# A cached-attention decode kernel: the output projection moved behind the last V piece, V sums gathered before they are turned, and one V piece loaded in two row ranges

## The chip, the cores and the metric

One NeuronCore of a Trainium2 chip; one launch. Times are device microseconds (us) of whole executions. Most are medians of 4 to 9 runs, taken in turns with the kernel before on the same chip. A program on one core has no second core to compare with, so single looks have an unknown state; all the runs behind a median were fast ones, and the granted TensorE clock is given where it matters.

## The reference

A decode step with a key/value cache (B = 4, one query token each, 32 heads, 8192 cached keys, head size 128, bf16), mixed by a gate with a small expert layer:

```python
q = (x @ wq)                                  # 4 x 32 heads x 128
scores = einsum("bhqd,bhkd->bhqk", q, k_cache) * 128**-0.5
p = softmax(scores)
o = einsum("bhqk,bhkd->bhqd", p, v_cache)
a = o.reshape(B, 1, 32 * 128) @ wo            # the output projection, wo is 4096 x 1024
b = x + scattered gated MLP(x)                # B_w_gate, B_w_up, B_w_down
out = g * a + (1 - g) * b
```

The caches K and V are 268 MB each. Everything is read once: 575.7 MB in all.

## The kernel before

K and V stream through a ring of five SBUF buffers in pieces of 4 MB (two heads of one batch entry, 128 partitions x 32 KB). There are NT = 64 K pieces and 64 V pieces; V trails K by LAG = 4. `V[NT-1]` below is the last V piece.

```python
HT = 2; JR = 128; GT = 4; GH = 8; NT = 64; LAG = 4; RING = JR * Dh      # 16384 elements
ring = ctx.enter_context(tc.tile_pool(name="ring", bufs=5))
...
def kv_view(cache, u):
    b, h0 = heads(u)
    return cache[b, h0:h0 + HT].rearrange("h (r j) d -> (h r) (j d)", j=JR)   # 128 rows of 32 KB
...
def v_piece(u):
    ...
    vn = slot()                                   # the next ring buffer
    vv = kv_view(A_v_cache, u)
    cut = 4 if u == NT - 1 else 1                 # the last piece comes in 4 column cuts
    for c in range(cut):
        lo, hi = c * RING // cut, (c + 1) * RING // cut
        nc.sync.dma_start(out=vn[:, lo:hi], in_=vv[:, lo:hi])
    o_ps = ops.tile([NM, 4 * Dh], F32, name="o_ps")            # NM = 8 rows
    ...                                           # 32 matmuls of 128x512 into o_ps
    o_sb = osp.tile([NM, 4 * Dh], F32, name="o_sb")
    nc.scalar.copy(out=o_sb[:], in_=o_ps[:])
    def finish():                                 # turn this piece's sums
        ...
        for q in range(4):
            nc.tensor.matmul(oT[:, HT * t:HT * t + HT], lhsT=o_sb[:, q * Dh:(q + 1) * Dh],
                             rhs=ident[0:NM, q:NM:4], start=(q == 0), stop=(q == 3))
        if t == GT - 1: ...                       # every 4th piece: scale into OT
    pending.append(finish)                        # run inside the next piece
...
GE = NWB - GH // WB                               # 6 of 8 row groups of wo, known before the last group
GS = GE // 2 + 1                                  # 4
for u in range(NT + LAG):
    if u < NT: k_piece(u)
    if u == NT + 1:
        flush(); o_rows(0, GE)
        wo_piece(0, GS)()                         # 4 MB of wo, between V[NT-4] and V[NT-3]
    if u >= LAG: v_piece(u - LAG)
    ...
early = wo_piece(GS, GE)                          # 2 MB, loaded behind V[NT-1]
late = [wo_piece(GE, NWB - 1), wo_piece(NWB - 1, NWB, 0, FR - 1), wo_piece(NWB - 1, NWB, FR - 1, FR)]
flush(); early(); o_rows(GE, NWB)
for use in late: use()
...                                               # acc -> res -> out
```

`wo_piece` issues a load and returns the matmuls that use it (8 of 128x512 per row group); `o_rows` turns finished heads into the projection's stationary rows.

Of the kernel before, what the change touches and what calls it, by code (L numbers as in the profile page):

```python
# [10 lines left out]
F32 = mybir.dt.float32  # L11
U32 = mybir.dt.uint32
ACT = mybir.ActivationFunctionType
ALU = mybir.AluOpType
# [5 lines left out]
def kernel(  # L20
# [22 lines left out]
    nc = tc.nc  # L43
    P = 128
    Bn, Sq, D = A_x.shape
    _, H, Sk, Dh = A_k_cache.shape
    F = B_w_gate.shape[1]
    DT = D // P
    HT = 2
    JR = Sk * HT // P  # L50
    JC = JR // 16
    GT = 4
    GH = GT * HT
# [3 lines left out]
    NT = Bn * H // HT  # L57
    LAG = 4
    FR = 4
# [3 lines left out]
    RING = JR * Dh  # L63
# [6 lines left out]
    const = ctx.enter_context(tc.tile_pool(name="const", bufs=1))  # L70
    ring = ctx.enter_context(tc.tile_pool(name="ring", bufs=5))
    ttp = ctx.enter_context(tc.tile_pool(name="ttp", bufs=2))
    ptp = ctx.enter_context(tc.tile_pool(name="ptp", bufs=2))
    osp = ctx.enter_context(tc.tile_pool(name="osp", bufs=2))
    stat = ctx.enter_context(tc.tile_pool(name="stat", bufs=3))
    shrp = ctx.enter_context(tc.tile_pool(name="shrp", bufs=1, space=PSUM))
    accp = ctx.enter_context(tc.tile_pool(name="accp", bufs=1, space=PSUM))
# [1 line left out]
    ops = ctx.enter_context(tc.tile_pool(name="ops", bufs=2, space=PSUM))  # L79
    o2p = ctx.enter_context(tc.tile_pool(name="o2p", bufs=1, space=PSUM))  # L80

    def slot():
        return ring.tile([P, RING], BF, name="piece", tag="piece")
# [11 lines left out]
    ident = const.tile([P, P], F32)  # L95
# [11 lines left out]
    for he in range(4):  # L107
        half, e = divmod(he, 2)
        nc.gpsimd.affine_select(out=R[:, he, :], in_=R[:, he, :], compare_op=ALU.not_equal, fill=1.0,  # L109
                                base=-(64 * half + e), pattern=[[0, 4], [-2, 32]], channel_multiplier=1)  # L110
# [3 lines left out]
                            base=0, pattern=[[-JC, GT], [-32, NQ]], channel_multiplier=1)  # L114
    nc.gpsimd.affine_select(out=m32[:], in_=m32[:], compare_op=ALU.is_ge, fill=0.0,
                            base=JC - 1, pattern=[[JC, GT], [32, NQ]], channel_multiplier=-1)
# [3 lines left out]
    nc.vector.tensor_scalar(out=pen8[:], in0=mask8[:], scalar1=-1.0, scalar2=3.0e38, op0=ALU.add, op1=ALU.mult)  # L120
    nmask8 = const.tile([P, GH], F32)
    nc.vector.tensor_scalar(out=nmask8[:], in0=mask8[:], scalar1=-scale, scalar2=None, op0=ALU.mult)
    ZW = 31 + P + 1
    Zt = [const.tile([P, 4, ZW], BF, name=f"Z{i}") for i in range(2)]
    PB = [const.tile([P, 32, 4, HT, 4], BF, name=f"PB{i}") for i in range(2)]
    for z in Zt + PB:
        nc.gpsimd.memset(z[:], 0.0)  # L127

    qT = const.tile([P, H, Bn], BF)
# [1 line left out]
    OT = const.tile([P, H, Bn], BF)  # L131
    LT = const.tile([P, FR, H // FR, Bn], BF)
    hT = const.tile([P, FG, FR, Bn], BF)
    sgb = const.tile([P, 2, Bn], F32)
# [10 lines left out]
    def mm_acc(out_ap, lhsT, rhs, start=False):  # L145
        nc.tensor.matmul(out_ap, lhsT=lhsT, rhs=rhs, start=start, stop=True, skip_group_check=True)  # L146
# [67 lines left out]
    NWB = H // WB  # L214

    def o_rows(g0, g1):

        n = g1 - g0
        lp = ops.tile([P, FR, n, Bn], F32, name="o_ps")
        for k in range(WB):  # L220
            for r in range(FR):
                nc.tensor.matmul(lp[32 * k:32 * k + 32, r], lhsT=identb[:, r:P:FR],
                                 rhs=OT[:, WB * g0 + k:WB * g1:WB, :], start=True, stop=True, skip_group_check=True)
        nc.vector.tensor_copy(out=LT[:, :, g0:g1, :], in_=lp[:])

    def wo_piece(g0, g1, r0=0, r1=FR):
        ng, nr = g1 - g0, r1 - r0
        w = slot()[:, :ng * nr * D].rearrange("p (g r n) -> p g r n", g=ng, r=nr)
        nc.sync.dma_start(out=w.rearrange("p g r n -> p g (r n)"),
                          in_=wov[:, g0:g1, r0:r1].rearrange("p g r n -> p g (r n)"))  # L230

        def use():
            for g in range(ng):
                for r in range(nr):
                    for n in range(NH):
                        mm_acc(acc[:, n * NB:(n + 1) * NB], LT[:, r0 + r, g0 + g, :], w[:, g, r, n * NB:(n + 1) * NB])
        return use
# [1 line left out]

    S_ps = {}  # L240
    rinv_t = {}
    oT_t = {}
    pending = []

    def flush():
        while pending:
            pending.pop(0)()

    def heads(u):
        return divmod(u * HT, H)  # L250

    def kv_view(cache, u):
        b, h0 = heads(u)
        return cache[b, h0:h0 + HT].rearrange("h (r j) d -> (h r) (j d)", j=JR)

    def k_piece(u):
        b, h0 = heads(u)
        g, t = divmod(u, GT)
        Z = Zt[u % 2]
        for a in range(NQ):  # L260
            nc.gpsimd.tensor_copy(out=Z[32 * a:32 * a + 32, :, 31 + 32 * a:32 + 32 * a],  # L261
                                  in_=qa[32 * a:32 * a + 32, :, h0 + a // QH, b:b + 1])
        if t == 0:
            S_ps[g] = scp.tile([P, 512], F32, name="S_ps")
        sps = S_ps[g]
        kn = slot()
        nc.sync.dma_start(out=kn[:], in_=kv_view(A_k_cache, u))
        for c in range(JR // CJ):
            T = ttp.tile([P, CJ, 2, 32, 2], BF, name="T", tag="T")
            nc.vector.transpose(out=T[:].rearrange("p j h i e -> p (j h i e)").bitcast(U32),  # L270
                                in_=kn[:, c * CJ * Dh:(c + 1) * CJ * Dh].bitcast(U32))
            for jl in range(CJ // 16):
                jc = c * (CJ // 16) + jl
                s = 31 - (JC * t + jc)
                for he in range(4):
                    half, e = divmod(he, 2)
                    nc.tensor.matmul(sps[:, :], lhsT=Z[:, he, s:s + P], rhs=T[:, 16 * jl:16 * jl + 16, half, :, e],  # L277
                                     start=(t == 0 and jc == 0 and he == 0),
                                     stop=(t == GT - 1 and jc == JC - 1 and he == 3))
            if c == 0:  # L280
                flush()
        if t == GT - 1:
            softmax(g)
# [32 lines left out]
    NM = 4 * HT  # L316

    def v_piece(u):
        b, h0 = heads(u)
        g, t = divmod(u, GT)  # L320
        B_ = PB[g % 2]
        vn = slot()
        vv = kv_view(A_v_cache, u)
        cut = 4 if u == NT - 1 else 1
        for c in range(cut):
            lo, hi = c * RING // cut, (c + 1) * RING // cut
            nc.sync.dma_start(out=vn[:, lo:hi], in_=vv[:, lo:hi])
        o_ps = ops.tile([NM, 4 * Dh], F32, name="o_ps")
        n = 0
        for jc in range(JC):  # L330
            for uq in range(4):
                j0 = 16 * jc + 4 * uq
                nc.tensor.matmul(o_ps[:, :], lhsT=B_[:, JC * t + jc, uq].rearrange("p s j -> p (s j)"),  # L333
                                 rhs=vn[:, j0 * Dh:(j0 + 4) * Dh], start=(n == 0), stop=(n == JR // 4 - 1))
                n += 1
                if n == 8:
                    flush()
        o_sb = osp.tile([NM, 4 * Dh], F32, name="o_sb")
        nc.scalar.copy(out=o_sb[:], in_=o_ps[:])  # L339

        def finish():
            if t == 0:
                oT_t[g] = o2p.tile([P, GH], F32, name="oT")
            oT = oT_t[g]
            for q in range(4):
                nc.tensor.matmul(oT[:, HT * t:HT * t + HT], lhsT=o_sb[:, q * Dh:(q + 1) * Dh],  # L346
                                 rhs=ident[0:NM, q:NM:4], start=(q == 0), stop=(q == 3))
            if t == GT - 1:
                oT_t.pop(g)
                hg = h0 + HT - GH  # L350
                nc.vector.scalar_tensor_tensor(out=OT[:, hg:hg + GH, b], in0=oT[:, :], scalar=sgb[:, 1, b:b + 1],  # L351
                                               in1=rinv_t.pop(g)[:], op0=ALU.mult, op1=ALU.mult)
        pending.append(finish)


# [4 lines left out]
    side = [lambda: gu_piece(wgv, 0, 0), lambda: gu_piece(wgv, 0, TW), lambda: gu_piece(wuv, 1, 0),  # L360
            lambda: (gu_piece(wuv, 1, TW), h_done()), lambda: wd_piece(0, 4), lambda: wd_piece(4, FG - 4)]
    GE = NWB - GH // WB
    GS = GE // 2 + 1
    for u in range(NT + LAG):
        if u < NT:
            k_piece(u)
        if u == NT + 1:
            flush()
            o_rows(0, GE)
            wo_piece(0, GS)()  # L370
        if u >= LAG:
            v_piece(u - LAG)
        if side:
            side.pop(0)()
    early = wo_piece(GS, GE)
    late = [wo_piece(GE, NWB - 1), wo_piece(NWB - 1, NWB, 0, FR - 1), wo_piece(NWB - 1, NWB, FR - 1, FR)]
    flush()
    early()
    o_rows(GE, NWB)
    for use in late:  # L380
        use()
    res = const.tile([Bn, D], BF)
    nc.vector.tensor_copy(out=res[:, 0:NB], in_=acc[:, 0:NB])
# [33 lines left out]
```

## Time and profile before

| | before |
|---|---|
| time, median of 4 runs | 1356.68 us |
| span of the profiled run | 1354.7 us |
| bytes loaded | 575.7 MB, steadily 430 GB/s |
| TensorE busy | 83% |
| VectorE busy | 46% |

The first lines come from the page of the kernel before: TensorE's busy time (PE matmuls, PEld weight loads, with their counts), then the span in 40 slices of 33.9 us, as the busy share of the 16 DMA engines in tenths and as the rate that they moved, then the queue of instruction transfers (count, MB, share).

```profile
...
PE 1119.6 (83%) x5496; PEld 483.1 (36%) x5496; DVE 624.2 (46%) x403; ACT 71.0 (5%) x118; POOL 85.2 (6%) x322
...
DMA  9999999999999999999999999999999999999996
GB/s 404 428 432 427 427 432 430 433 431 429 430 431 430 433 431 430 429 432 431 430 433 431 430 431 430 429 432 432 431 433 431 432 428 429 431 432 433 432 422 257
...
q8 instruction: 43, 0.70, 0.2%
...
```

The load stream is the limit: every slice but the first and the last two runs at 427 to 433 GB/s, and 575.7 MB at 432 GB/s alone take 1333 us. Only some 22 us of the span lie outside.

The table by stretches, kernel before, last 60 us. The second line names the columns; the last three are the granted TensorE clock, the mean busy share of the DMA engines and the rate.

```profile
...
core 0: us, PE busy (x) PEld busy (x) DVE busy (x) ACT busy (x) POOL busy (x), PEclk, DMA share, GB/s
...
1300.00:1310.00 10.00, 8.46 (x58) 4.13 (x57) 0.26 (x1) 0.57 (x1) 0.00 (x0) 1.00 1.02 437
1310.00:1320.00 10.00, 7.35 (x29) 2.57 (x27) 0.00 (x0) 0.00 (x0) 0.00 (x0) 0.84 1.01 433
1320.00:1334.00 14.00, 13.28 (x65) 5.75 (x64) 0.00 (x0) 0.57 (x1) 0.00 (x0) 1.00 0.98 409
...
1340.00:1350.00 10.00, 8.96 (x61) 4.14 (x59) 0.43 (x2) 0.57 (x1) 0.00 (x0) 1.00 0.27 109
...
```

The stream keeps its rate until the loads run out. The timeline of the tail, kernel before (start, duration, engine, line, operation, idle time before it):

```profile
...
1317.20 8.50 PE L333 MATMUL o_ps<-piece,PB_139 128*8 128x512 bf16 x32 [2.65 <-DMA piece<-in_A_v_cache_dram]
...
1327.40 8.80 PE L333 MATMUL o_ps<-piece,PB_139 128*8 128x512 bf16 x40
...
1337.10 5.34 PE L333 MATMUL o_ps<-piece,PB_139 128*8 128x512 bf16 x24
...
1344.88 6.85 PE L146 MATMUL acc<-piece,LT 128*4 128x512 bf16 x31
...
1351.77 0.57 ACT L385 CAST res<-acc 4x512 bf16<-4x512 f32 x1 [8.65 <-PE acc L146]
...
```

V[NT-3] lands at 1317.2, V[NT-2] at 1326.9 (landing records of the trace), the last cut of V[NT-1] at 1336.8, the last of `wo` at 1346.8. From 1317 on TensorE is the later of the two: it reads three V pieces, turns their sums, then runs 32 projection matmuls (1344.9 to 1351.7); 3 us of evacuation and output follow.

One more reading needs the landing records, not a view: the 16 DMA engines do not stand at the same place. In the trace each full load has 16 arrivals on its semaphore, read here as one per engine. For the last load before the end they lie between 1337.3 and 1346.8 us, so the engines are 9.5 us apart.

### The profile page before, as it was taken

Reading aid. Unit: us, or ns where it says so; the run is one execution under the profiler, and the core shown is the slowest. Engines: PE = TensorE matmul, PEld = TensorE weight load, DVE = VectorE, ACT = ScalarE, POOL = GpSimd, SP = SyncE. Lnnn points to the kernel's source line nnn. Section 1 sums busy time; section 2 is a strip of 40 time slices with the busy share of each in tenths; the row PEclk is TensorE's granted clock in tenths of the full one; section 3 lists DMA queues with packets and bytes.
Section 4 is the critical chain, followed back from the end, with each engine's and each line's share of the span. In section 5 each row is a group of like instructions: output and inputs, shape, how many; then the busy total and the mean of one; then the engine's idle time right before and its main releaser. Section 6 shows DMA issues by size and latency. Waiting matters only on the chain.

```text
span 1354.7 us, 12547 instructions
## 1 busy us (share of the span) xinstructions
PE 1119.6 (83%) x5496; PEld 483.1 (36%) x5496; DVE 624.2 (46%) x403; ACT 71.0 (5%) x118; POOL 85.2 (6%) x322
## 2 busy tenths in 40 slices
PE   3765988888787988888888888888888887888888
PEld 2432433333333333333333333333333333333333
DVE  1553445544554454455445534554454445445500
ACT  0001000000000000000000000000000000000000
POOL 1000000000000000000000000000000000000000
PEclk9877989899999998989998999989989999998999
DMA  9999999999999999999999999999999999999996
GB/s 404 428 432 427 427 432 430 433 431 429 430 431 430 433 431 430 429 432 431 430 433 431 430 431 430 429 432 432 431 433 431 432 428 429 431 432 433 432 422 257
DMA packets 21971, 576.50 MB, mean 426 GB/s; under 512 B 2318, under 2 KB 2326, under 8 KB 2588
## 3 DMA queue, kind: packets, MB, share of 16 engines
q1 hardware_dynamic: 21896, 575.68, 99.0%
q8 instruction: 43, 0.70, 0.2%
q14 instruction: 12, 0.10, 0.0%
q10 hardware_dynamic: 20, 0.02, 0.0%
HBM read 575.68 MB, written 0.01 MB: 425 GB/s over the span
## 4 chain that ended last, share of the span: by engine, by line
DMA 48%; PE 33%; DVE 11%; issue 7%; ACT 1%; POOL 0%; DVEq 0%; ACTq 0%; POOLq 0%
DMA piece<-in_A_k_cache_dram 45%; PE o_ps L333 17%; PE S_ps L277 13%; DVE T L270 10%; DMA piece<-in_A_v_cache_dram 3%; PE acc L146 1%; PE oT L346 1%; PE shr L146 1%; ACT o_sb L339 1%; DVE OT L351 0%; DVE xf L159 0%; POOL Z_137 L127 0%; POOL R L109 0%; POOL PB_138 L307 0%; DVEq L270 0%
## 5 line engine op out<-in xcount | busy, mean ns | idle before, releaser
L270 DVE STREAM_TRANSPOSE T<-piece 128x2048 uint32<-128x2048 uint32 x256 | 577.5, 2291 | 506.8 <-DMA piece<-in_A_k_cache_dram 380.7
L277 PE MATMUL S_ps<-T,Z_136 128*128 128x512 bf16 x1024 | 283.6, 431 | 102.2 <-DVE T L270 102.0
L277 PE MATMUL S_ps<-T,Z_137 128*128 128x512 bf16 x1024 | 266.1, 410 | 60.2 <-DVE T L270 60.1
L333 PE MATMUL o_ps<-piece,PB_139 128*8 128x512 bf16 x1024 | 227.7, 381 | 2.7 <-DMA piece<-in_A_v_cache_dram 2.7
L333 PE MATMUL o_ps<-piece,PB_138 128*8 128x512 bf16 x1024 | 226.2, 379 | 0.0
L277 PEld LDWEIGHTS <-Z_136 128*128 128x128 bf16 x1024 | 109.4, 107 | 264.0 <-issue 180.4
L277 PEld LDWEIGHTS <-Z_137 128*128 128x128 bf16 x1024 | 104.3, 103 | 208.8 <-issue 116.9
L333 PEld LDWEIGHTS <-PB_139 128*8 128x8 bf16 x1024 | 86.7, 87 | 139.9 <-issue 16.9
L333 PEld LDWEIGHTS <-PB_138 128*8 128x8 bf16 x1024 | 86.4, 87 | 137.3 <-issue 13.6
L346 PE MATMUL oT<-ident,o_sb 8*128 8x2 f32 x512 | 67.1, 249 | 45.0 <-ACT o_sb L339 45.0
L346 PEld LDWEIGHTS oT<-ident,o_sb 8*128 8x128 f32 x512 | 61.6, 186 | 76.8 <-ACT o_sb L339 76.4
L339 ACT COPY o_sb<-o_ps 8x512 f32<-8x512 f32 x64 | 36.8, 575 | 943.0 <-PE o_ps L333 943.0
L261 POOL COPY Z_137<-qa 32x4 bf16<-32x4 bf16 x128 | 24.9, 194 | 558.1 <-PE S_ps L277 552.5
L261 POOL COPY Z_136<-qa 32x4 bf16<-32x4 bf16 x128 | 24.9, 195 | 554.3 <-PE S_ps L277 533.6
L351 DVE SCALAR_TENSOR_TENSOR OT<-oT,sgb,rinv 128x8 bf16<-128x8 f32 x16 | 3.8, 236 | 90.2 <-PE oT L346 90.2
L146 PEld LDWEIGHTS <-piece 128*128 128x128 bf16 x704 | 22.5, 113 | 4.4 <-issue 3.5
L146 PE MATMUL shr<-xw,piece 128*128 128x4 bf16 x704 | 22.6, 170 | 1.7 <-issue 1.7
L300 ACT ACTIVATE PTs<-S_ps,negm 128x512 bf16<-128x512 f32 x16 | 11.0, 687 | 215.0 <-DVE negm L297 215.0
L302 DVE STREAM_TRANSPOSE PT<-PTs 128x512 bf16<-128x512 bf16 x16 | 11.4, 711 | 13.5 <-ACT PTs L300 13.5
L146 PE MATMUL acc<-piece,LT 128*4 128x512 bf16 x64 | 14.1, 379 | 1.0 <-DMA piece<-in_A_wo_dram 1.0
L313 DVE RECIPROCAL rinv<-tot 128x8 f32<-128x8 f32 x16 | 3.2, 203 | 25.3 <-POOL tot L311 25.3
L146 PE MATMUL acc<-piece,hT 128*4 128x512 bf16 x56 | 12.4, 379 | 0.0
(92 smaller groups left out, 111.0 us busy)
## 6 DMA issues: line engine op xcount, KB each, us to landing
piece<-in_A_k_cache_dram SPq DMA_DIRECT2D x64, 4096.0 KB, 39.2
piece<-in_A_v_cache_dram SPq DMA_DIRECT2D x63, 4096.0 KB, 39.2
piece<-in_A_wq_dram SPq DMA_DIRECT2D x2, 4096.0 KB, 13.1
piece<-in_B_w_gate_dram SPq DMA_DIRECT2D x2, 3584.0 KB, 40.0
piece<-in_B_w_up_dram SPq DMA_DIRECT2D x2, 3584.0 KB
piece<-in_B_w_down_dram SPq DMA_DIRECT2D x1, 4096.0 KB, 39.6
piece<-in_A_wo_dram SPq DMA_DIRECT2D x1, 4096.0 KB
piece<-in_A_v_cache_dram SPq DMA_DIRECT2D x4, 1024.0 KB, 38.5
```

Of the source, the lines that this page charges most:

```text
L146: nc.tensor.matmul(out_ap, lhsT=lhsT, rhs=rhs, start=start, stop=True, skip_group_check=True)
L261: nc.gpsimd.tensor_copy(out=Z[32 * a:32 * a + 32, :, 31 + 32 * a:32 + 32 * a], in_=qa[32 * a:32 * a + 32, :, h0 + a // QH, b:b + 1])
L270: nc.vector.transpose(out=T[:].rearrange("p j h i e -> p (j h i e)").bitcast(U32), in_=kn[:, c * CJ * Dh:(c + 1) * CJ * Dh].bitcast(U32))
L277: nc.tensor.matmul(sps[:, :], lhsT=Z[:, he, s:s + P], rhs=T[:, 16 * jl:16 * jl + 16, half, :, e], start=(t == 0 and jc == 0 and he == 0), ...
L300: nc.scalar.activation(out=PTs[:], in_=sps[:], func=ACT.Exp, bias=negm[:, 0:1], scale=scale, accum_out=rs[:, 0:1])
L302: nc.vector.transpose(out=PT[:].rearrange("p j i -> p (j i)"), in_=PTs[:])
L313: nc.vector.reciprocal(out=rinv[:], in_=tot[:])
L333: nc.tensor.matmul(o_ps[:, :], lhsT=B_[:, JC * t + jc, uq].rearrange("p s j -> p (s j)"), rhs=vn[:, j0 * Dh:(j0 + 4) * Dh], start=(n == 0) ...
L339: nc.scalar.copy(out=o_sb[:], in_=o_ps[:])
L346: nc.tensor.matmul(oT[:, HT * t:HT * t + HT], lhsT=o_sb[:, q * Dh:(q + 1) * Dh], rhs=ident[0:NM, q:NM:4], start=(q == 0), stop=(q == 3))
L351: nc.vector.scalar_tensor_tensor(out=OT[:, hg:hg + GH, b], in0=oT[:, :], scalar=sgb[:, 1, b:b + 1], in1=rinv_t.pop(g)[:], op0=ALU.mult, op ...
```

## The change

Three intents: (1) all of `wo` streams behind V, so that V's serial tail (sum, copy, turn, scale) hides under 8 MB of loads; (2) the sums of four V pieces gather in one 128-partition tile, at partitions 0, 32, 64 and 96, and are turned once per group, which removes 48 of 64 turnings; (3) V[NT-2] is loaded as 120 + 8 partitions, to give one DMA engine less.

```diff
+    selg = const.tile([P, 4, GT, HT], F32)            # selector for gathered sums
+    ...
+    OS = [const.tile([P, 4 * Dh], F32, name=f"OS{i}") for i in range(2)]
...
-        cut = 4 if u == NT - 1 else 1
-        for c in range(cut):
-            ...
-        o_ps = ops.tile([NM, 4 * Dh], F32, name="o_ps")
+        if u == NT - 2:
+            nc.sync.dma_start(out=vn[0:120], in_=vv[0:120])
+            nc.sync.dma_start(out=vn[120:P], in_=vv[120:P])
+        else:
+            cut = 4 if u == NT - 1 else 1
+            ...                                       # as before
+        o_ps = ops.tile([P, 4 * Dh], F32, name="o_ps")
...
-                nc.tensor.matmul(o_ps[:, :], lhsT=..., rhs=...)
+                nc.tensor.matmul(o_ps[32 * t:32 * t + NM, :], lhsT=..., rhs=...)
-        o_sb = osp.tile([NM, 4 * Dh], F32, name="o_sb")
-        nc.scalar.copy(out=o_sb[:], in_=o_ps[:])
+        o_sb = OS[g % 2]
+        nc.scalar.copy(out=o_sb[32 * t:32 * t + NM, :], in_=o_ps[32 * t:32 * t + NM, :])
+        if t < GT - 1:
+            return
         def finish():
-            ... 4 matmuls per piece
+            oT = o2p.tile([P, GH], F32, name="oT")
             for q in range(4):
-                nc.tensor.matmul(oT[:, HT * t:HT * t + HT], ..., rhs=ident[0:NM, q:NM:4], ...)
+                nc.tensor.matmul(oT[:, :], ..., rhs=selg[:, q].rearrange("p t s -> p (t s)"), ...)
...
-        if u == NT + 1:
-            flush()
-            o_rows(0, GE)
-            wo_piece(0, GS)()
         if u >= LAG:
             v_piece(u - LAG)
+        if u == NT:
+            o_rows(0, GE)
-    early = wo_piece(GS, GE)
-    late = [...]
-    flush(); early(); o_rows(GE, NWB)
+    GS = NWB // 2
+    last = [wo_piece(0, GS), wo_piece(GS, GE), wo_piece(GE, NWB - 1),        # 4, 2, 1 MB
+            wo_piece(NWB - 1, NWB, 0, FR - 1), wo_piece(NWB - 1, NWB, FR - 1, FR)]   # 0.75, 0.25 MB
+    flush(); o_rows(GE, NWB)
```

More of the change, by code (lines that the diff above doesn't have):

```diff
@@ L73 @@
     ptp = ctx.enter_context(tc.tile_pool(name="ptp", bufs=2))
-    osp = ctx.enter_context(tc.tile_pool(name="osp", bufs=2))
     stat = ctx.enter_context(tc.tile_pool(name="stat", bufs=3))
@@ L122 @@
     nc.vector.tensor_scalar(out=nmask8[:], in0=mask8[:], scalar1=-scale, scalar2=None, op0=ALU.mult)
+    selg = const.tile([P, 4, GT, HT], F32)
+    nc.gpsimd.memset(selg[:], 0.0)
+    nc.gpsimd.affine_select(out=selg[:], in_=selg[:], compare_op=ALU.not_equal, fill=1.0,
+                            base=0, pattern=[[-1, 4], [-32, GT], [-4, HT]], channel_multiplier=1)
+    OS = [const.tile([P, 4 * Dh], F32, name=f"OS{i}") for i in range(2)]
     ZW = 31 + P + 1
@@ L125 @@
     PB = [const.tile([P, 32, 4, HT, 4], BF, name=f"PB{i}") for i in range(2)]
-    for z in Zt + PB:
+    for z in Zt + PB + OS:
         nc.gpsimd.memset(z[:], 0.0)
@@ L241 @@
     rinv_t = {}
-    oT_t = {}
     pending = []
@@ L323, in v_piece @@
         vv = kv_view(A_v_cache, u)
-        cut = 4 if u == NT - 1 else 1
-        for c in range(cut):
-            lo, hi = c * RING // cut, (c + 1) * RING // cut
-            nc.sync.dma_start(out=vn[:, lo:hi], in_=vv[:, lo:hi])
-        o_ps = ops.tile([NM, 4 * Dh], F32, name="o_ps")
+        if u == NT - 2:
[3 more added lines that the diff above has]
+            cut = 4 if u == NT - 1 else 1
+            for c in range(cut):
+                lo, hi = c * RING // cut, (c + 1) * RING // cut
+                nc.sync.dma_start(out=vn[:, lo:hi], in_=vv[:, lo:hi])
+        o_ps = ops.tile([P, 4 * Dh], F32, name="o_ps")
         n = 0
@@ L332, in v_piece @@
                 j0 = 16 * jc + 4 * uq
-                nc.tensor.matmul(o_ps[:, :], lhsT=B_[:, JC * t + jc, uq].rearrange("p s j -> p (s j)"),
+                nc.tensor.matmul(o_ps[32 * t:32 * t + NM, :], lhsT=B_[:, JC * t + jc, uq].rearrange("p s j -> p (s j)"),
                                  rhs=vn[:, j0 * Dh:(j0 + 4) * Dh], start=(n == 0), stop=(n == JR // 4 - 1))
@@ L337, in v_piece @@
                     flush()
-        o_sb = osp.tile([NM, 4 * Dh], F32, name="o_sb")
-        nc.scalar.copy(out=o_sb[:], in_=o_ps[:])
+        o_sb = OS[g % 2]
+        nc.scalar.copy(out=o_sb[32 * t:32 * t + NM, :], in_=o_ps[32 * t:32 * t + NM, :])
+        if t < GT - 1:
+            return
         def finish():
-            if t == 0:
-                oT_t[g] = o2p.tile([P, GH], F32, name="oT")
-            oT = oT_t[g]
+            oT = o2p.tile([P, GH], F32, name="oT")
             for q in range(4):
-                nc.tensor.matmul(oT[:, HT * t:HT * t + HT], lhsT=o_sb[:, q * Dh:(q + 1) * Dh],
-                                 rhs=ident[0:NM, q:NM:4], start=(q == 0), stop=(q == 3))
-            if t == GT - 1:
-                oT_t.pop(g)
-                hg = h0 + HT - GH
-                nc.vector.scalar_tensor_tensor(out=OT[:, hg:hg + GH, b], in0=oT[:, :], scalar=sgb[:, 1, b:b + 1],
-                                               in1=rinv_t.pop(g)[:], op0=ALU.mult, op1=ALU.mult)
+                nc.tensor.matmul(oT[:, :], lhsT=o_sb[:, q * Dh:(q + 1) * Dh],
+                                 rhs=selg[:, q].rearrange("p t s -> p (t s)"), start=(q == 0), stop=(q == 3))
+            hg = h0 + HT - GH
+            nc.vector.scalar_tensor_tensor(out=OT[:, hg:hg + GH, b], in0=oT[:, :], scalar=sgb[:, 1, b:b + 1],
+                                           in1=rinv_t.pop(g)[:], op0=ALU.mult, op1=ALU.mult)
         pending.append(finish)
@@ L362 @@
     GE = NWB - GH // WB
-    GS = GE // 2 + 1
     for u in range(NT + LAG):
@@ L374 @@
             side.pop(0)()
-    early = wo_piece(GS, GE)
-    late = [wo_piece(GE, NWB - 1), wo_piece(NWB - 1, NWB, 0, FR - 1), wo_piece(NWB - 1, NWB, FR - 1, FR)]
+        if u == NT:
[3 more added lines that the diff above has]
+            wo_piece(NWB - 1, NWB, 0, FR - 1), wo_piece(NWB - 1, NWB, FR - 1, FR)]
     flush()
-    early()
     o_rows(GE, NWB)
-    for use in late:
+    for use in last:
         use()
```

## The prediction

The sum of the forecast: 0.7 us from the order (step 1), 1.0 taken out of the 0 to 1.6 of step 2, zero from the split (step 3), together 1.7 us off 1355.9. The pages and records give both: 43 transfers ("blocks" in the text) to 10,992 TensorE records before, so 256 to one and three to 768 (an estimate from these counts), and, for the split, 15 arrivals for the 120 rows and 8 for the 8 rows, read as one per engine. The 9.7 and 1.2 us are eight and one times the 1.21 us of a 32 KB packet.

> **What bounds it.** The load stream. The page counts 576.5 MB at a mean 426 GB/s; nearly every slice shows 427 to 433 GB/s, DMA engines 90% busy or more. 4 MB pieces land every 9.71 us (432 GB/s), and 575.7 MB at that rate is about 1333 us of the 1354.7 us span. Only some 22 us (1.6%) lie outside: about 2.5 us before the first bytes, and the tail. TensorE (83% busy) and VectorE (46%) keep ahead of it until the end.
>
> **The tail before** (timeline, chain of waits, landings). V[NT-3] lands at 1317.2, V[NT-2] at 1326.9, the last quarter of V[NT-1] at 1336.8, `wo` at 1341.7, 1344.2, 1346.1, 1346.8. After V[NT-2], TensorE is the limit: it reads V[NT-2] and V[NT-1] until 1342.5 (7.07 us each, and 1.05 us of turning), then copy, turn, scale and rows until 1344.9, then 32 projection matmuls until 1351.7 (6.87 us, 0.22 us each), then evacuation and output, 3 us.
>
> **What the change does.**
> 1. Order. The first 4 MB of `wo` move behind V[NT-1], so every late V piece lands 9.71 us earlier: last quarter about 1327.1. TensorE finishes it at about 1332.5 (it now trails V[NT-2], landing at 1317.2), and turn and rows at about 1335. The first 4 MB of `wo` land at about 1336.8, and 64 matmuls follow it: 64 x 0.22 = 14.2 us, to 1351.0, against 1351.7 before. V's exposed tail shrinks, the projection's grows from 32 to 64 matmuls, all waiting for one 4 MB load. Gain 0.7 us.
> 2. Turning once per group: 48 turnings of 1.05 us (50 us of TensorE) go, nearly all off the critical path, as the stream is the limit. But each turning is 16 TensorE records here (8 matmul, 8 weight load): 768 fewer instructions. The trace shows 42 instruction transfers of 16 KB before the last data, and by the landing times one of the 16 engines falls back about 1.6 us per transfer; two engines end at 1346.7, a cluster at 1345.0. [...] With 39 blocks no engine should have the sixth, so late landings come about 1.6 us earlier. Estimated gain 0 to 1.6 us.
> 3. Split V[NT-2], 120 + 8 partitions. [...] one engine is spared 8 rows (9.7 us), eight take one more (1.2 us). If the spared one is the straggler this helps by up to 1.6 us; if stragglers are among the eight, it costs 1.2. I take zero.
> 4. Setup fits into GpSimd's idle time (19 to 34 us).
>
> **Prediction.** TensorE ends at about 1350, the span at 1353.0, and the median time, 1355.9 less 1.7, at 1354.2 us, 8 in 10 within 1351.8 to 1356.2. Faster by over 2%: 0.01; within 2%: 0.98; slower by over 2%: 0.01.
>
> **What would show it.** Steady 9.71 us per piece unchanged; 64 projection matmuls unbroken after the first 4 MB of `wo`, landing at 1335 to 1337; V's sums done before that; TensorE's busy time about 50 us lower; about 40 instruction transfers; the spread of the 16 engines at the last landing smaller than now (1337.3 to 1346.8).
>
> **What would make it wrong.** The split running on far fewer engines (+5 to 10 us); the last 256 KB of `wo`, whose buffer waits for the first 4 MB to be used, landing late; TensorE starting the 64 matmuls at a lower clock (+1.5 us); the fetch pattern falling otherwise than counted.

## The result, and the profile after

1375.80 us (1374.92 to 1376.29, 4 runs) against 1356.68 us: 19 us slower, outside the predicted range. Ratios in this document are the mean time of one kernel's fast runs over the mean of the other's fast runs of the same rounds, so they are not quite the ratios of the medians quoted beside them; here 1.0140, 95% interval 1.0122 to 1.0157. That is under 2%, and far outside the noise.

The page of the kernel after, the same lines as above (slices of 34.4 us):

```profile
...
PE 1079.0 (78%) x5112; PEld 437.7 (32%) x5112; DVE 623.5 (45%) x403; ACT 71.0 (5%) x118; POOL 86.2 (6%) x326
...
DMA  9999999999999999999999999999999999999995
GB/s 403 431 430 428 428 434 430 431 431 431 431 429 432 431 430 432 432 431 429 431 433 431 429 434 431 431 430 434 430 428 431 435 429 429 435 430 430 384 241 236
...
q8 instruction: 40, 0.66, 0.2%
...
```

Nothing changed in the first 37 slices. Then the rate falls to 384, 241 and 236 GB/s, while the DMA engines stay as busy as ever. That is the point to notice: a busy DMA engine here is one that holds a packet (92 to 103% of the time at 201 to 210 GB/s, below), not one that moves bytes at full rate. Two side readings: 384 fewer matmul and 384 fewer weight-load records, and 40 instruction transfers instead of 43, as predicted.

By stretches, kernel after, the same columns:

```profile
...
1290.00:1298.00 8.00, 5.49 (x29) 2.58 (x27) 0.96 (x3) 2.22 (x4) 0.77 (x1) 0.99 1.03 436
...
1300.00:1310.00 10.00, 7.02 (x45) 2.83 (x43) 0.26 (x1) 0.57 (x1) 0.00 (x0) 0.93 1.00 210
1310.00:1320.00 10.00, 6.64 (x20) 2.18 (x21) 0.00 (x0) 0.00 (x0) 0.00 (x0) 0.66 1.03 206
1320.00:1334.00 14.00, 2.90 (x14) 0.97 (x12) 0.00 (x0) 0.58 (x1) 0.00 (x0) 0.69 0.92 201
1334.00:1340.00 6.00, 3.40 (x9) 1.07 (x10) 0.00 (x0) 0.00 (x0) 0.00 (x0) 0.50 0.99 399
1340.00:1350.00 10.00, 10.00 (x47) 3.85 (x46) 0.00 (x0) 0.58 (x1) 0.00 (x0) 0.89 0.99 412
...
```

From about 1299 to 1334 us, 35 us long, the stream runs at 201 to 210 GB/s with 92 to 103% busy DMA engines. At 428 GB/s the same bytes take 17 us: the loss is 18 us, nearly all of the 19 to be explained. In the packet records a 32 KB packet takes 2.5 us there instead of 1.21 us, and an 8 KB packet 0.65 instead of 0.31. All through the stretch some 16 packets are in flight (15 to 18, mean 16.1), so no engine stands idle for long.

The timeline of the tail, kernel after (the two loads of the split piece are the lines that begin with 1276; the last line is the whole projection):

```profile
...
1276.18 0.41 SPq L328 DMA_DIRECT2D piece<-in_A_v_cache_dram  x1
...
1276.64 0.28 SPq L329 DMA_DIRECT2D piece<-in_A_v_cache_dram  x1
...
1313.36 9.54 PE L340 MATMUL o_ps<-piece,PB_143 128*8 128x512 bf16 x32 [6.34 <-DMA piece<-in_A_v_cache_dram]
...
1336.60 15.91 PE L340 MATMUL o_ps<-piece,PB_143 128*8 128x512 bf16 x64 [13.70 <-DMA piece<-in_A_v_cache_dram]
...
1356.10 15.56 PE L150 MATMUL acc<-piece,LT 128*4 128x512 bf16 x64 [1.15 <-DMA piece<-in_A_wo_dram]
...
```

V[NT-3] now lands at 1313.3 (6.3 us of idle TensorE before it) and V[NT-2], the split piece, at 1336.5 (13.7 us idle). Had nothing slowed, they would have landed near 1306 and 1315, as a run below shows.

The landing records name the time at which it begins. The 16 engines finish V[NT-3] one after another, at 1297.6, 1297.8, 1298.0, 1298.6, 1298.9 and so on to 1313.3; fifteen of them then enter the split piece, and the spared one goes on to V[NT-1]. All lengthening packets but two point to one onset, about 1298.9, and from then on the packets of all 16 engines are slow, also of those that are still in V[NT-3]. The other two packets lengthen alone, from about 1297.9 (to 1.85 and 2.08 us), while the rest still keep 1.22 us. The packet records of b_split, a_src36 and a_mid, below, show the same two steps: first two packets alone, then, 0.7 to 1.3 us later, all engines at once. The landing records also show 15 arrivals for the 120-row load and 8 for the 8-row load, where a full load has 16.

### The profile page after: what moved, and what is told of

Read it like the earlier page. It is cut to its first block, busy times and chain, and to the rows that moved or that the text cites. A ratio compares the mean times of both kernels' runs of the same rounds, so it can differ in the third digit from the quotient of the medians.

```text
span 1374.6 us, 11810 instructions
## 1 busy us (share of the span) xinstructions
PE 1079.0 (78%) x5112; PEld 437.7 (32%) x5112; DVE 623.5 (45%) x403; ACT 71.0 (5%) x118; POOL 86.2 (6%) x326
## 4 chain that ended last, share of the span: by engine, by line
DMA 43%; PE 35%; DVE 12%; issue 6%; POOL 2%; another core or an unknown queue 1%; ACT 1%; DVEq 0%; ACTq 0%; POOLq 0%
DMA piece<-in_A_k_cache_dram 39%; PE o_ps L340 17%; PE S_ps L280 14%; DVE T L273 10%; DMA piece<-in_A_v_cache_dram 3%; PE acc L150 2%; PE shr L150 1%; PE oT L353 1%; DVE PT L305 1%; POOL PB_142 L310 1%; POOL PB_143 L310 0%; POOL tot L314 0%; ACT OS_139 L346 0%; DVE xf L163 0%
## 5 line engine op out<-in xcount | busy, mean ns | idle before, releaser
L346 ACT COPY OS_138<-o_ps 8x512 f32<-8x512 f32 x32 | 18.5, 577 | 594.0 <-PE o_ps L340 594.0
L346 ACT COPY OS_139<-o_ps 8x512 f32<-8x512 f32 x32 | 18.5, 577 | 560.8 <-PE o_ps L340 560.8
L353 PE MATMUL oT<-selg,OS_138 128*128 128x8 f32 x64 | 8.5, 259 | 5.7 <-ACT OS_138 L346 5.7
L353 PE MATMUL oT<-selg,OS_139 128*128 128x8 f32 x64 | 8.5, 259 | 5.7 <-ACT OS_139 L346 5.7
L310 POOL COPY PB_143<-PT 64x512 bf16<-64x512 bf16 x8 | 8.2, 1026 | 66.0 <-DVE rex L312 66.0
```

Source lines behind the costliest of these rows:

```text
L310: nc.gpsimd.tensor_copy(out=B_[W:P, :, :, 1, :], in_=Pv[W:P])
L346: nc.scalar.copy(out=o_sb[32 * t:32 * t + NM, :], in_=o_ps[32 * t:32 * t + NM, :])
L353: nc.tensor.matmul(oT[:, :], lhsT=o_sb[:, q * Dh:(q + 1) * Dh], rhs=selg[:, q].rearrange("p t s -> p (t s)"), start=(q == 0), stop=(q == 3))
```

## The experiments

The theory: the split of V[NT-2] by rows slows the whole stream while it is in flight. The rival: the new order (8 MB of `wo` behind V) or the gathered sums do it.

Overview; "ratio" is against the kernel before of the same rounds, "before" its median.

| run | time, us | before, us | ratio (95%) |
|---|---|---|---|
| the change | 1375.80 | 1356.68 | 1.0140 (1.0122 to 1.0157) |
| a_whole: change without the split | 1356.46 | 1357.59 | 0.9992 (0.9978 to 1.0005) |
| b_split: before with the split | 1377.97 | 1357.59 | 1.0149 (1.0136 to 1.0163) |
| a_rows64: split 64+64 rows | 1374.68 | 1357.59 | 1.0126 (1.0112 to 1.0140) |
| a_cols: split by columns | 1355.80 | 1357.59 | 0.9989 (0.9975 to 1.0002) |
| a_rows32: four row ranges | 1373.77 | 1358.82 | 1.0116 (1.0101 to 1.0131) |
| a_rows16: eight row ranges | 1379.14 | 1358.82 | 1.0152 (1.0135 to 1.0169) |
| a_src36: split, other source rows | 1377.79 | one look | - |
| a_src64: whole, source rows apart | 1355.74 | one look | - |
| a_mid: split at V[20] | 1375.75 | 1357.28 | 1.0140 (1.0123 to 1.0157) |
| b_gather: before with gathering | 1354.18 | 1356.38 | 0.9982 (0.9969 to 0.9994) |
| b_order: before with the new order | 1357.62 | 1356.38 | 1.0006 (0.9993 to 1.0018) |
| a_warm: a_whole, TensorE kept busy | 1354.38 | 1356.38 | 0.9980 (0.9968 to 0.9993) |
| a_wo2: a_whole, 2 MB pieces of `wo` | 1351.97 | 1356.38 | 0.9963 (0.9950 to 0.9977) |

All kernels passed the comparison with the reference, also the seven that load wrong or missing data (a_src36, a_src64, a_port2, a_port4, a_port8, a_port16 and the control a_rot8 leave one of 64 V pieces wrong). That comparison can't see one wrong V piece, so it proves little for them.

### a_whole: take the split out of the change

```diff
-        if u == NT - 2:
-            nc.sync.dma_start(out=vn[0:120], in_=vv[0:120])
-            nc.sync.dma_start(out=vn[120:P], in_=vv[120:P])
-        else:
+        # V[NT-2] in one DMA of 128 partitions again
```

> The changed kernel with V[NT-2] loaded by one DMA of 128 partitions again; everything else of the change stays. Theory (the 120+8 row split halves the whole stream while it is in flight): the slow stretch of 208 GB/s disappears and the time falls from 1375.8 to 1352-1356 us. Rival (the new order: 8 MB of wo queued behind V, or the gathered sums, slows the tail): stays at 1370-1377 us.

1356.46 us: 19 us gone, 0.5 us above the expected range. The rate line of its page:

```profile
...
GB/s 404 429 432 427 427 431 431 431 432 430 433 429 431 433 430 430 431 430 431 432 431 432 433 431 432 428 430 430 431 433 433 433 430 431 429 429 430 433 423 251
...
```

The slow slices are gone. V[NT-3], V[NT-2] and V[NT-1] land at 1305.6, 1315.4 and 1325.3 (landing records). The rival falls: order and gathering together change the time by less than the noise.

### b_split: put the split alone into the kernel before

```diff
+        if u == NT - 2:
+            nc.sync.dma_start(out=vn[0:120], in_=vv[0:120])
+            nc.sync.dma_start(out=vn[120:P], in_=vv[120:P])
+        else: ...
```

> The kernel before with only the 120+8 split of V[NT-2]. Theory: 17 to 21 us slower than before (1373-1378 us), with a stretch of some 35 us at about 208 GB/s in which packets of 32 KB take 2.5 us instead of 1.21. Rival (order or gathering): no change, 1355-1358 us.

1377.97 us, ratio 1.0149; two slices at 208 and 202 GB/s on its page:

```profile
...
GB/s 402 430 433 426 429 432 430 432 432 430 430 434 428 431 433 429 431 434 429 431 433 431 428 434 432 428 432 433 428 431 436 427 431 434 429 431 432 427 208 202
...
```

So the split costs some 20 us in either kernel, and it is the only part that costs.

### a_rows64, a_cols: what about the split is slow?

```diff
-            nc.sync.dma_start(out=vn[0:120], in_=vv[0:120])
-            nc.sync.dma_start(out=vn[120:P], in_=vv[120:P])
+            # a_rows64: vn[0:64], then vn[64:128]
+            # a_cols:   vn[:, 0:RING//2], then vn[:, RING//2:RING]   (128 partitions each)
```

"Port theory" is the name for the guess that what counts is which partitions an engine writes, and "pitch theory" for the guess that source rows at some distances from each other are read slowly.

> The changed kernel with V[NT-2] split 64+64 rows. Tells why the split is slow. Port theory (which partition an engine writes[...]): as slow as 120+8 or nearly, 1368-1377 us, packets near 2.4 us. Engine-count theory (15 and 8 engines, uneven shares): all 16 engines work evenly, so no loss, 1352-1357 us. [...]

> The changed kernel with V[NT-2] split in two by columns, 128 partitions each. Port theory, pitch theory and engine-count theory: no loss, 1352-1356 us[...]. Rival (two DMAs in the place of one are themselves slow): part of the 20 us loss remains.

64+64 rows, an even cut, are nearly as slow as 120+8 (1374.68 us), with DMA engines 94 to 103% busy in the stretches below. Two column halves, also two DMAs, cost nothing (1355.80 us). So neither an uneven cut nor a second DMA is what it takes; what the slow runs have in common is a DMA that spans fewer than 128 partitions. Stretches of a_rows64:

```profile
...
1300.00:1310.00 10.00, 6.93 (x45) 2.81 (x43) 0.26 (x1) 0.57 (x1) 0.00 (x0) 0.95 1.03 223
...
1320.00:1334.00 14.00, 2.97 (x14) 1.04 (x12) 0.00 (x0) 0.58 (x1) 0.00 (x0) 0.80 0.94 208
...
```

The rates, 223 and 208 GB/s, are half of the usual 430. Loads which are not part of the split slow down with it, too; see below.

### a_src36, a_src64: is it the source instead?

Which source rows an engine reads, and how far apart, no record shows; so the distances between the rows are changed. Other distances, same destination; then the whole-piece load with distances doubled:

```diff
+            ws = A_v_cache.rearrange("b h s d -> (b h s d)")[0:P * (RING + 2048)].rearrange("(p c) -> p c", p=P)
+            nc.sync.dma_start(out=vn[0:120], in_=ws[0:120, 0:RING])       # a_src36, rows 36 KB apart
+            nc.sync.dma_start(out=vn[120:P], in_=ws[120:P, 0:RING])
+            # a_src64: one DMA of 128 partitions, source rows 64 KB apart
```

> The changed kernel with its 120+8 split kept, but the rows of V[NT-2] read from source addresses 36 KB apart instead of 32 KB (wrong data, on purpose: the result fails). Port theory (what matters is where the rows are written): as slow as the change, 1372-1378 us, 32 KB packets near 2.5 us. Pitch theory (source rows collide in HBM): the loss shrinks or goes, 1353-1360 us.

> The changed kernel with V[NT-2] in one DMA of 128 partitions, its source rows 64 KB apart (wrong data, on purpose: the result fails). Pitch theory: [...] it is slow, 1365-1377 us. Port theory: no loss, 1354-1358 us.

1377.79 us with the split and 1355.74 us without it: the distance between source rows does not matter, the destination rows do. (Single looks, of unknown state; the difference, 22 us, is far more than the 3.3 us over which the kernel before spread in the same call.)

### a_rows32, a_rows16: fewer partitions per DMA

```diff
+            for p0 in range(0, P, 32):                                    # a_rows16: steps of 16
+                nc.sync.dma_start(out=vn[p0:p0 + 32], in_=vv[p0:p0 + 32])
```

> The changed kernel with V[NT-2] in four DMAs of 32 partitions[...]. Port theory: [...] the same half rate and the same loss as 64+64: 1371-1378 us. Theory of loss per DMA (each smaller DMA costs): twice the DMAs, so about twice the loss of 64+64, 1385-1400 us.

> The changed kernel with V[NT-2] in eight DMAs of 16 partitions[...]. Port theory: [...] as engines stand up to 8 us (6 rows) apart they are in different DMAs, so anything between 18 and 53 us, 1374-1410 us, and slower than 32 rows. Theory of loss per DMA: see 32 rows, double again.

Four DMAs of 32 partitions cost the same as two of 64 (1.0116 and 1.0126), so the loss does not go by the number of DMAs. Eight DMAs of 16 partitions cost 5 us more (1379.14 us), at rates down to 171 GB/s:

```profile
...
1310.00:1320.00 10.00, 6.72 (x24) 2.40 (x25) 0.00 (x0) 0.00 (x0) 0.00 (x0) 0.67 0.96 180
1320.00:1334.00 14.00, 2.00 (x10) 0.61 (x7) 0.00 (x0) 0.58 (x1) 0.00 (x0) 0.75 0.94 171
...
```

The loss is at the low end of the expected range. The upper end, 53 us, reckoned with a quarter of the rate, which was not shown. The expectation's reason, that the engines stand in different DMAs at a time, fits, but was not tested by itself.

### a_mid: the same split in the middle of the run

```diff
-        if u == NT - 2:
+        if u == 20:
```

> The changed kernel with the 120+8 split moved from V[NT-2] to V[20], in the middle of the run. If the split's cost is the stream's (half rate from the first engine entering the piece to the last leaving it, with engines some 4 us apart there instead of 8): slow stretch (9.7+4) x 2 = 27 us, loss about 14 us against the whole-piece kernel: 1368-1373 us. If the cost needs the tail (its waits, the short pieces behind it): little loss, 1355-1359 us.

```profile
...
GB/s 403 431 429 428 428 432 431 431 431 430 429 435 430 428 411 228 433 431 431 429 431 433 429 431 432 431 430 430 431 430 434 430 429 433 433 428 429 434 421 254
...
```

1375.75 us, as slow as at the end. The cost is the stream's, anywhere; no later slack pays it back. My size was wrong (14 us expected, some 19 found): in the packet records the stretch lasts from about 511 to 543 us, 32 us instead of 27, and from 530 to 541 us, as the engines reach the 8-row load, the rate averages 155 GB/s, below half. I had counted the whole stretch at half rate.

### a_port2, a_port4, a_port8, a_port16, a_rot8: why do all 16 engines slow?

Each of these loads the first half of V[NT-2]'s columns as usual, zeroes the second half, and loads only a few rows of it, so that 2, 4 or more engines write a few partitions at a time. V[NT-1] and the rest of the first half are the bystanders. By the landing records the small loads of a_port2, a_port4 and a_port8 ran on 2, 4 and 8 engines. The author picked the partitions on the assumption that those of one group meet at one place, a "port"; that is not shown, and "port" is only a name here.

```diff
+            hf = RING // 2
+            nc.sync.dma_start(out=vn[:, 0:hf], in_=vv[:, 0:hf])
+            nc.gpsimd.memset(vn[:, hf:RING], 0.0)
+            for p0 in (0, 2, 32, 34):                       # a_port2: 2 partitions each
+                nc.sync.dma_start(out=vn[p0:p0 + 2, hf:RING], in_=vv[p0:p0 + 2, hf:RING])
+            # a_port4:  partitions 0-3 and 32-35 in four DMAs of 4 (half of these columns each)
+            # a_port8:  p0 in (0, 8, 32, 40), 8 partitions each
+            # a_port16: p0 in (0, 16, 32, 48), 16 partitions each
+            # a_rot8:   vn[p0:p0 + 29:4] for p0 in (4, 5, 6, 7): 8 partitions each, 4 apart
```

> The changed kernel; of V[NT-2] the first half of the columns comes in one DMA of 128 partitions, the second half is zeroed and then loaded for partitions 0-3 and 32-35 alone, by four DMAs of 2 partitions (2 engines each; wrong data, on purpose). [...] If a crowded port slows only those who write to it: packets of two engines take about double for some 3 to 6 us, the other fourteen keep 1.21 us per 32 KB and 0.31 us per 8 KB. If a crowded port holds up the whole stream: packets of all 16 engines take longer in that stretch, total rate near 208 GB/s or lower for 3 to 6 us. Time itself tells little (2 MB less is loaded): 1349-1356 us.

> As a_port2 (half of V[NT-2] missing on purpose), but partitions 0-3 and 32-35 come by four DMAs of 4 partitions[...]. Simple sharing: packets of those four take about 4 times as long (8 KB 1.2 us instead of 0.31) for about 5 us, the other twelve keep 0.31 us. Stream-wide hold-up from some number of writers on: the others' packets lengthen too.

> As a_port2, but partitions 0-15 and 32-47 come by four DMAs of 8 partitions[...]. Simple sharing: packets of these eight take about 4 times as long (16 KB 2.4 us instead of 0.61), the other eight keep 0.31 us per 8 KB. Hold-up of the whole stream: the others lengthen too.

> As a_port2, but partitions 0-63 come by four DMAs of 16 partitions[...]. If any crowding just halves the stream: about 210 GB/s, 1.25 us.

> Control: as a_port2, but partitions 4, 8, ... 32 (then 5, 9, ... 33 and so on) come by four DMAs of 8 partitions with a step of 4[...]. Port crowding theory: no packet lengthens (16 KB stay at 0.61 us). [...]

Their times, 1354.47, 1352.85, 1358.62, 1360.72 and 1355.56 us in this order, matter little, as 1 to 2 MB less is loaded; what counts is the rate in the stretch.

Stretches of a_port4 (before, during and after its small loads), then of a_port2, a_port8 and a_port16 during their own. The first line is low (267 GB/s at a DMA share of 0.63) for another reason: the small loads, and all loads behind them on the queue, were issued only when GpSimd had zeroed the second half, at 1305.7, so some engines had run out of work.

```profile
...
1302.00:1307.00 5.00, 5.00 (x38) 2.07 (x38) 0.00 (x0) 0.00 (x0) 3.67 (x1) 1.00 0.63 267
1308.00:1310.50 2.50, 2.50 (x13) 0.99 (x12) 0.00 (x0) 0.00 (x0) 0.00 (x0) 1.00 0.93 118
1312.00:1315.00 3.00, 3.00 (x20) 1.24 (x18) 0.00 (x0) 0.10 (x1) 0.00 (x0) 1.00 1.00 410
...
```

```profile
...
1309.80:1312.80 3.00, 3.00 (x16) 1.20 (x15) 0.00 (x0) 0.00 (x0) 0.00 (x0) 1.00 0.96 371
...
```

```profile
...
1308.00:1317.00 9.00, 9.00 (x47) 3.69 (x44) 0.00 (x0) 0.58 (x1) 0.00 (x0) 1.00 0.95 217
...
```

```profile
...
1309.00:1318.00 9.00, 9.00 (x46) 3.61 (x46) 0.00 (x0) 0.58 (x1) 0.00 (x0) 1.00 0.99 170
...
```

With two engines at a time on partitions 0 to 3 and 32 to 35 (a_port2) these two take 1.28 us for 16 KB instead of 0.61, most of the other fourteen keep 0.31 us per 8 KB, and the total is 371 GB/s. With four on the same partitions (a_port4) the total falls to 118 GB/s, and the bystanders are held up as well: 16 KB packets of the first half, which belong to engines outside the small loads, take up to 2.4 us instead of 0.61. So loads of a few partitions can slow the whole stream: the four writers did (118 GB/s) and the two hardly (371 GB/s), each run a single look. a_port8 and a_port16 show the same for longer (rates from the packet records, us by us): 187 to 271 GB/s and 149 to 197 GB/s, for some 9 us each, both stream-wide, in place of the 4-fold packets of eight engines alone that simple sharing gave for a_port8. (The factor of four there and in a_port4 was the author's guess.) The control, a_rot8, writes eight partitions 4 apart in each DMA. It was not clean: its packets were to keep 0.61 us and took 0.7 to 0.9 on average, at 250 to 290 GB/s in all. That rate says little, as on average only 11 to 16 packets were in flight (before its small loads the stream stood at 241 GB/s with nine). Why the packets lengthened was not tested, and a_rot8 settles nothing.

### b_gather, b_order: the two other parts, each alone

```diff
# b_gather: kernel before + OS, selg, gathered turning; wo in the order of before
# b_order:  kernel before + o_rows(0, GE) after V[NT-4], all wo behind V, 4 MB first; turning per piece
```

> The kernel before with the V sums gathered and turned once a group alone: order of wo and whole loads as before. Instruction transfers fall from 42 to about 39, which frees the slowest DMA engines of one transfer each (1.6 us): V[NT-3], V[NT-2] and V[NT-1] land about 1.6 us earlier, TensorE's last turnings (about 1 us) go too. Expect 1.6 to 2.8 us less than before. Rival (steady state hides it all, and so does the tail): within 0.5 us of before.

> The kernel before with the new order of wo alone (all of it behind the last V piece, 4 MB first), turning per piece as before, whole loads. First wo piece lands at 1336.8 as no instruction transfer is saved; TensorE idles before it, 64 matmuls at a clock that starts low take 16.6 us: ends at 1353.4, 1.7 us later than before. Expect +0.5 to +2.5 us against before. If it is faster than before, the order itself is the gain.

Gathering alone gains 2.2 us by the medians (0.9982). The last load lands at 1345.2 instead of 1346.8, in a_whole as well (1345.2), and not in b_order (1346.6): it goes with the 40 instead of 43 instruction transfers. The order alone gains nothing (1.0006, with one in the interval). The timeline of b_order shows its projection in one block:

```profile
...
1336.64 16.23 PE L146 MATMUL acc<-piece,LT 128*4 128x512 bf16 x64 [1.82 <-DMA piece<-in_A_wo_dram]
...
```

16.2 us for 64 matmuls, near the 16.6 that was expected of a clock that starts low; at 0.22 each, as the prediction of the change had it, they would take 14.1.

### a_warm, a_wo2: where the order's gain went, and a better version

In a_whole the first `wo` load of 4 MB lands at 1335.3, and TensorE has been idle for 4.3 us. The stretches of a_whole (clock in the third column from the end) and its projection:

```profile
...
1331.00:1335.30 4.30, 0.01 (x1) 0.00 (x0) 0.19 (x1) 0.00 (x0) 0.00 (x0) 0.84 1.01 420
1335.30:1339.00 3.70, 3.69 (x9) 1.11 (x9) 0.00 (x0) 0.00 (x0) 0.00 (x0) 0.50 0.85 353
...
1340.00:1341.00 1.00, 1.00 (x5) 0.31 (x4) 0.00 (x0) 0.00 (x0) 0.00 (x0) 0.64 0.61 244
1341.00:1345.00 4.00, 4.00 (x20) 1.60 (x19) 0.00 (x0) 0.00 (x0) 0.00 (x0) 1.00 0.45 179
...
```

```profile
...
1335.31 16.63 PE L150 MATMUL acc<-piece,LT 128*4 128x512 bf16 x64 [4.30 <-DMA piece<-in_A_wo_dram]
...
```

The granted clock is 0.50 for the first 5 us of the projection, and the 64 matmuls take 16.6 us. Two ways to avoid it:

```diff
# a_warm: a_whole + after o_rows(GE, NWB)
+    dm = ops.tile([P, 512], F32, name="o_ps")
+    for i in range(14):                          # results unused
+        nc.tensor.matmul(dm[:, :], lhsT=identb[:], rhs=<512 columns of PB[0]>, start=True, stop=True)
# a_wo2: a_whole with
-    GS = NWB // 2
-    last = [wo_piece(0, GS), wo_piece(GS, GE), ...]                       # 4, 2, 1, 0.75, 0.25 MB
+    GS = NWB // 4
+    last = [wo_piece(0, GS), wo_piece(GS, 2 * GS), wo_piece(2 * GS, GE), ...]   # 2, 2, 2, 1, 0.75, 0.25 MB
```

> The changed kernel without the split, with 14 idle matmuls of 128x512 between the rows and the first use of wo. If the lower granted clock (0.50 for about 5 us after an idle 4.3 us) is what made 64 matmuls take 16.6 us instead of 14.2, they now take about 14.2 and the time falls by about 2.4 us, to 1353.5-1355 us. If the clock does not follow TensorE's activity: no change, 1356-1357 us.

> The changed kernel without the split, and with wo in pieces of 2, 2, 2, 1, 0.75 and 0.25 MB instead of 4, 2, 1, 0.75, 0.25. The first piece lands at about 1330.4 us, just as TensorE has the rows ready (1331), so TensorE does not idle 4.3 us, keeps its full clock, and follows the stream: last load at 1345.2, last projection matmul at about 1346 instead of 1351.9. Expect 5 us less than the whole-piece kernel: 1350-1352.5 us. Rival (the tail is set by the stream or by something else than the wait for 4 MB): no change, 1355-1357 us.

The timelines of a_warm, then of a_wo2:

```profile
...
1331.03 4.88 PE L380 MATMUL o_ps<-PB,identb 128*128 128x512 bf16 x14
...
1335.84 13.97 PE L150 MATMUL acc<-piece,LT 128*4 128x512 bf16 x64
...
```

```profile
...
1330.99 8.54 PE L150 MATMUL acc<-piece,LT 128*4 128x512 bf16 x31
...
1340.23 7.07 PE L150 MATMUL acc<-piece,LT 128*4 128x512 bf16 x32 [0.71 <-DMA piece<-in_A_wo_dram]
...
1347.34 0.57 ACT L383 CAST res<-acc 4x512 bf16<-4x512 f32 x1 [18.12 <-PE acc L150]
...
```

With fourteen idle matmuls ahead of it, the same projection takes 13.97 us, and the time is 1354.38 us. (a_whole was timed in another call, and the two ratios' intervals overlap; the size of this gain rests on the traces, 13.97 us against 16.63.) The low clock is not gone: by the clock records it is granted from 1331.4 to 1334.8, during the idle matmuls, which therefore take 4.88 us. With 2 MB pieces TensorE goes straight from the last V rows into the projection, follows the stream, and ends at 1347.3: 1351.97 us, 0.37% under the kernel before (0.9963, interval 0.9950 to 0.9977), the fastest of all versions. Here, too, one part of the expectation failed: TensorE did not keep its full clock, though it did not idle. The stretch of a_wo2:

```profile
...
1331.40:1334.80 3.40, 3.40 (x9) 1.03 (x8) 0.00 (x0) 0.00 (x0) 0.00 (x0) 0.50 1.01 419
...
```

So eight of the first 31 matmuls start about 0.4 us apart instead of 0.22, and the 31 take 8.5 us, with no wait among them. This costs nothing here, as TensorE still waits 0.71 us for the third piece, which lands at 1340.2; the 32 matmuls behind it set the end (1347.3 where about 1346 was expected), 2.1 us after the last load at 1345.2.

## Why the prediction was wrong, point by point

- **"The load stream" bounds the kernel, 9.71 us per 4 MB piece: right.** It stayed so for 37 slices. That is also why the mistake could not be absorbed.
- **Step 3, the split: wrong, and it is the step that failed.** The text took "I take zero" for it, between a gain of 1.6 us and a cost of 1.2 us. Measured: about +20 us (b_split 1.0149 against before; change 1.0140 against a_whole 0.9992). The shares were right: 15 and 8 engines, as the landing records show. But the step counted rows per engine and took the rate of each engine as given, whatever partitions a load spans. What the runs show is that the whole stream falls to 201 to 210 GB/s for 35 us, a loss of 18 us where the piece alone, at half rate, would lose 9.7 (an estimate from the 9.71 us per piece). Why is not shown; see the last point.
- The spared engine wasn't the straggler either. The short packets of V[NT-1] begin at 1297.5, when the very first engine leaves V[NT-3]; so the engine that was given less was the one farthest ahead.
- **"The split running on far fewer engines (+5 to 10 us)": the wrong worry.** Some 16 packets were in flight all through (15 to 18); the engines were slow, not idle, and the loss was twice the size.
- **Step 2, fewer instruction transfers: right.** 43 became 40 on the page, with 768 fewer TensorE records (10,992 before, 10,224 after, 256 to a transfer in both). By the landing records of the kernel before, the 16 arrivals of a load lie 1.3 us apart at the start and 9.5 us at the end; from 460 us on this grows by about 1.5 us at every eighth transfer (4.9, 6.4, 8.0, 9.5 us). The last load of a_whole and b_gather lands 1.6 us earlier than that of before. b_gather gained 2.2 us; 0 to 1.6 was predicted from this step, and part of the rest is the turnings that left the tail. The smaller spread of the engines at the last landing came only without the split: 8.0 us in a_whole against 9.5 before, but 11.2 in the change.
- **Step 1, the order: mechanism right, size wrong.** The first 4 MB of `wo` landed at 1335.3 in a_whole (1335 to 1337 predicted) and V's sums were done before it. But "64 x 0.22 = 14.2 us" was 16.6 us, because TensorE started at half its clock after idling 4.3 us (13 matmuls some 0.4 us apart). The text had this only as a risk ("+1.5 us"). By the clock records the low stretch lasted 6.8 us there, about 5 us of it in the projection, and 3.4 us in a_wo2, where TensorE did not idle; what starts and ends it was not shown. a_warm shows the size: 13.97 us, once the low clock falls on idle matmuls.
- Without the split the prediction of 1354.2 would have met 1356.46 us: 2.3 us off, just outside its range, and mostly the clock (16.6 us against 14.2). Against the kernel before (1357.59) the gain was 1.1 us, not clear of the noise, where 1.7 was predicted.
- **TensorE's busy time "about 50 us lower": 41 us lower**, as slower matmuls in the starved tail took some of it back; 46 us in a_whole.
- Not settled: why two engines on eight partitions leave most of the others alone (371 GB/s in a_port2) while four hold the stream at about a quarter of its rate (118 GB/s in a_port4), and why the row splits 120+8 and 64+64 both settle near half (201 to 223 GB/s). That the row splits are slow through the partitions that they write is supported by the source test (a_src36, a_src64), by the column halves (a_cols) and by a_port4, but the control a_rot8 was not clean, so the mechanism is not shown.

## What to carry to other kernels

In a kernel that streams from memory, keep every large load at 128 partitions and cut it by columns: two column halves cost nothing here (0.9989), a cut by rows halved the whole stream (201 to 210 GB/s of 430), other loads included, and cost just as much in the middle of the run (1.0140). When a rate falls while the DMA engines stay busy, look at the length of equal packets, not at busy shares. And where work is moved behind a load, let the first load be small enough that TensorE needn't wait for it: the wait of 4.3 us here went with another 2.7 us lost to the low clock (16.63 us against 13.97).
